# FNet and GEGLU layers on one core: when the last pair's wide tiles of x are loaded, and when the late norms run

## The chip, the core and the metric

The kernel runs on one core of a Trainium2 chip. Its time is the device time of one launch in microseconds; the median of three runs of the kernel before is 1612.08 us (1611.62 to 1616.12). TensorE (PE) multiplies, VectorE (DVE) and ScalarE (ACT) do the elementwise work, GpSimd (POOL) issues stores and some loads, and SyncE (SP) issues most loads. Each of these engines takes its instructions in the order in which they stand in its own program.

## What is computed

```python
x = A_x                                     # [1, 2048, 512], float32
for layer in range(2):
    z = layernorm(x)                        # over the 512 columns
    a = z @ dft_hid_re.T
    b = z @ dft_hid_im.T
    x = x + (dft_seq_re @ a - dft_seq_im @ b)       # FNet mixing, 2048 x 2048 matrices
    z = layernorm(x)
    x = x + (gelu(z @ w_gate) * (z @ w_up)) @ w_down  # GEGLU, 512 -> 1792 -> 512
```

The kernel counts these as four layers: 0 and 2 mix, 1 and 3 are GEGLU. The change lies at the end of layer 2 and the beginning of layer 3.

## The kernel before

Every matmul is of float32 data cut into a high and a low half, so each product of 128 x 128 by 128 x 512 is three matmuls (L227 high by high, L228 high by low, L229 low by high). ACT makes the high half of an operand (L170, or L196 on another form), DVE the low half (L172, L198). A product can start when ACT's half is there, and its second matmul when DVE's is. Both matrix stages are done by seven-product schemes, so sums of blocks (L203, L207, L210 on DVE) stand ahead of many splits. PSUM has eight banks, which ACT copies out (L214) or copies to another bank as a seed (L221).

The 2048 rows of x are four blocks of 512. Data sits in 98 slots of 128 x 512 in SBUF, and in two wide tiles of 1 MB, `wide` and `xwide`, each of which holds one block. In layer 2 the blocks are worked in pairs, (0, 1) and (2, 3). A block's stages are S2 and S4, sequences of matmul steps over the sequence dimension; its matrices stream through the slots as loads `s<-ws` on SP, and the hidden matrices as `s<-wq`. After S4 of the second block of a pair the products of the pair with the hidden matrices follow; `PAIR_REST`, twelve of them, makes the last ones. For the last pair these twelve are put aside in `spare`, and layer 3 runs them one by one beside its own first passes. Their results are turned by L865 and added into the wide tiles (L210), which must hold the old x by then, and `pair_out` (L980) stores the tiles as the next layer's x. `pair_wide_load` (L977) loads a wide tile from x in four pieces, on SP. For the last pair, `xwide` is loaded in S2 of block 3 at step 14 and `wide` in S4 at step 5 (`WIDE_AT`). For the first pair both are loaded before its products.

Layer 3 starts with half of x (blocks 0 and 1) normed in turn: `z^T` of these rows must be there. That is done inside layer 2, since x of blocks 0 and 1 is known. A row tile is loaded ("L" in `NORM_STEPS`, L255 or L264), its mean and variance are taken on DVE (L645, L647, "A"), POOL makes the reciprocal root (L652), DVE the shift (L656), ACT norms (L689), and DVE turns it into `wide` (L782, "B"). After four tiles POOL stores `wide` to a scratch tensor t (L785), and the same queue fetches z^T back in pieces of 64 KB (L796, `s<-t`). Tiles 4 to 7 come first; tiles 0 to 3 are the four late ones. `NORM_STEPS` says which of these parts run at which step, `NORM_LATE` the parts that go to the head of the queue of S2 of block 3, and the fetches follow after `FETCH_AT` queue steps:

```python
queue.extend(late + [None] * (FETCH_AT - len(late) if paired else 14)
             + [run for fetch in later.pop("fetches") for run in (None, fetch)])
```

The code's order sets what is issued first on each engine only in part: a scheduler orders the instructions within their dependences. SP takes loads one after the other; a load goes out when its slot is free, and with eight loads under way it waits for the oldest. Layer 3's first weights are the loads `s<-wb` (L1345), in high and low halves.

## Time and profile before

| | |
|---|---|
| median of the runs | 1612.08 us (1611.62 to 1616.12, 3 runs) |
| profiled execution | 1612.12 us; its span is 1610.3 us, mean clock of TensorE 0.994 |
| busy | PE 1592.9 us, DVE 1189.7, ACT 880.8, POOL 315.6 |
| DMA | 432.80 MB, 269 GB/s over the span |

A busy PE isn't PE at its peak: a matmul counts as busy also when the clock is halved. So PE's time is read by stretches, from the granted clock, the number of matmuls and the waits. A wait is named by what came last: `PE p L227 <- ACT s L170` means that the matmul of line 227 waited for a split of line 170. DMA share is the busy share of the 16 DMA engines, and can pass 1.00 a little.

### The profile page before, as it was taken

What the parts mean: (1) busy time and instruction counts of PE and PEld (TensorE: products, weight loads), DVE (VectorE), ACT (ScalarE), POOL (GpSimd) and SP (SyncE); (2) the same over time, 40 slices, a digit from 0 to 9 for tenths busy, and PEclk for the clock granted to TensorE, in tenths of its full rate; (3) what the DMA queues carried; (4) which work ended last, traced back from release to release, by engine and by line L of the source; (5) the groups of instructions that cost most, each with busy time, mean ns of one, the idle gap of its engine ahead of it and who ended that gap; (6) DMA issues with size and microseconds to landing.
All of it is one profiled execution on the core that took longest, in us unless ns stands there. A gap on an engine that the chain in (4) does not pass through costs nothing. (4 is left out here: it accounts for less than half of the span.)

```text
span 1610.3 us, 22765 instructions
## 1 busy us (share of the span) xinstructions
PE 1592.9 (99%) x6960; PEld 1311.8 (81%) x6960; DVE 1189.7 (74%) x2082; ACT 880.8 (55%) x1687; POOL 315.6 (20%) x533
## 2 busy tenths in 40 slices
PE   9999999999999999999999999999989999999999
PEld 7888888888888888888888888887768888888887
DVE  7997888878699784675878875998875556843574
ACT  8955565654767644656567543534542565433460
POOL 4122332341456102330040000022301000000000
PEclk9999999999999999999999999999889999999999
DMA  9888999976998899997786758789868958895445
GB/s 358 293 329 314 332 318 345 334 260 199 343 322 318 267 333 314 326 353 225 273 303 199 262 166 206 240 279 271 236 231 285 280 171 252 302 293 188 131 144 157
DMA packets 245019, 432.80 MB, mean 269 GB/s; under 512 B 29024, under 2 KB 72288, under 8 KB 243872
## 3 DMA queue, kind: packets, MB, share of 16 engines
q1 hardware_dynamic: 212208, 328.82, 63.6%
q0 software_dynamic: 30000, 100.43, 17.4%
q10 hardware_dynamic: 2688, 2.10, 0.5%
q8 instruction: 55, 0.90, 0.2%
q14 instruction: 68, 0.56, 0.1%
HBM read 333.97 MB, written 97.26 MB: 268 GB/s over the span
## 5 line engine op out<-in xcount | busy, mean ns | idle before, releaser
L228 PE MATMUL p<-s,s 128*128 128x512 f32 x2304 | 897.2, 390 | 0.6 <-DVE s L172 0.5
L229 PE MATMUL p<-s,s 128*128 128x512 f32 x2304 | 891.5, 390 | 3.5 <-DMA s<-wb 3.5
L227 PE MATMUL p<-s,s 128*128 128x512 f32 x2304 | 852.5, 391 | 8.3 <-ACT s L170 3.7
L170 ACT ACTIVATE s<-s 128x512 fp32r<-128x512 f32 (+1 forms) x852 | 480.4, 608 | 305.7 <-DVE s L203 69.7
L172 DVE TENSOR_TENSOR s<-s,s 128x512 fp32r<-128x512 f32 (+1 forms) x852 | 537.6, 663 | 119.5 <-ACT s L170 101.5
L227 PEld LDWEIGHTS p<-s,s 128*128 128x128 f32 x2304 | 434.2, 189 | 100.7 <-ACT s L170 4.7
L229 PEld LDWEIGHTS p<-s,s 128*128 128x128 f32 x2304 | 434.4, 189 | 94.1 <-DMA s<-wb 3.9
L228 PEld LDWEIGHTS p<-s,s 128*128 128x128 f32 x2304 | 434.1, 188 | 92.8 <-DVE s L172 2.2
L207 DVE TENSOR_TENSOR s<-s,p 128x512 f32<-128x512 f32 x211 | 142.3, 682 | 163.7 <-PE p L229 133.5
L203 DVE TENSOR_TENSOR s<-s,s 128x512 f32<-128x512 f32 (+1 forms) x399 | 234.6, 609 | 5.8 <-DMA s<-ws 3.2
L214 ACT ACTIVATE s<-p 128x512 f32<-128x512 f32 x234 | 135.6, 592 | 112.9 <-PE p L229 110.8
L1355 ACT ACTIVATE s<-s 128x512 f32<-128x512 f32 x84 | 52.8, 628 | 46.3 <-DVE s L207 45.9
L336 POOL DMA_DIRECT2D wb<-s x84 | 46.1, 550 | 86.2 <-ACT s L170 68.4
L1355 ACT ACTIVATE s<-p 128x512 f32<-128x512 f32 x28 | 16.7, 596 | 83.1 <-PE p L229 81.5
L689 ACT ACTIVATE s<-s,shift,rstd 128x512 f32<-128x512 f32 x61 | 48.8, 810 | 18.3 <-DVE shift L656 10.4
L1371 DVE TENSOR_TENSOR s<-s,p 128x512 f32<-128x512 f32 x56 | 38.3, 683 | 24.8 <-PE p L229 24.8
L980 POOL DMA_DIRECT2D x<-wide x8 | 5.2, 658 | 231.1 <-DVE wide L210 231.1
L221 ACT ACTIVATE p<-p 128x512 f32<-128x512 f32 x56 | 32.6, 584 | 31.6 <-PE p L229 31.4
L170 ACT ACTIVATE s<-xwide 128x512 fp32r<-128x512 f32 (+1 forms) x56 | 34.3, 618 | 27.9 <-DVE xwide L207 10.4
L210 DVE TENSOR_TENSOR s<-s,s 128x512 f32<-128x512 f32 (+1 forms) x61 | 36.4, 603 | 17.1 <-DMA s<-ws 12.4
L172 DVE TENSOR_TENSOR s<-xwide,s 128x512 fp32r<-128x512 f32 (+1 forms) x56 | 37.4, 676 | 15.3 <-ACT s L170 15.1
L666 POOL TENSOR_SCALAR rstd<-rstd 128x1 f32<-128x1 f32 x32 | 19.8, 619 | 108.1 <-ACT s L665 98.8
(96 smaller groups left out, 675.1 us busy)
## 6 DMA issues: line engine op xcount, KB each, us to landing
s<-ws SPq DMA_DIRECT2D x368, 256.0 KB, 5.0
s<-wb SPq DMA_DIRECT2D x294, 256.0 KB, 5.0
s<-wc SPq DMA_DIRECT2D x182, 256.0 KB, 4.4
wb<-s POOLq DMA_DIRECT2D x98, 256.0 KB, 4.6
s<-wq SPq DMA_DIRECT2D x56, 256.0 KB, 4.5
s<-x SPq DMA_DIRECT2D x52, 256.0 KB, 5.4
s<-wh SPq DMA_DIRECT2D x52, 256.0 KB, 5.6
wc<-s POOLq DMA_DIRECT2D x49, 256.0 KB, 5.4
```

What stands on the lines that cost most here:

```text
L170: newest["ACT"] = nc.scalar.activation(hi, src, AF.Copy)
L172: newest["DVE"] = nc.vector.tensor_tensor(lo, src, f32(hi), op=ALU.subtract)
L203: nc.vector.tensor_tensor(out, a, b, op=ALU.subtract)
L207: bank_read["DVE"] = nc.vector.tensor_tensor(out, a, b, op=ALU.add)
L214: bank_read["ACT"] = nc.scalar.activation(v, src, AF.Copy)
L227: nc.tensor.matmul(ps, ah, bh, start=start, stop=False, skip_group_check=True)
L228: nc.tensor.matmul(ps, ah, bl, start=False, stop=False, skip_group_check=True)
L229: newest["PE"] = nc.tensor.matmul(ps, al, bh, start=False, stop=stop, skip_group_check=True)
L336: nc.gpsimd.dma_start(a, f32(t))
L689: nc.scalar.activation(z, x, AF.Identity, bias=shift, scale=rstd)
L1355: nc.scalar.activation(t, g, AF.Gelu_apprx_tanh)
L1371: nc.vector.tensor_tensor(t, t, v, op=ALU.mult)
```

## The change

```diff
@@ -27,7 +27,7 @@
 MORE = 8
 RAW = 4
 FETCHING = 2
-WIDE_AT = 14, 5
+WIDE_AT = 0, 2
 IN_ORDER = (3, 0),
 HELD = {0: (1, 2, 3), 2: ()}
 WARM = 12
@@ -50,11 +50,11 @@
 BESIDE = 2
 FURTHER = 4
 NORM_STEPS = (
-    (("A", 4),), (("A", 5),), (("B", 4), ("A", 6)), (("B", 5), ("A", 7)), (("B", 6),), (("B", 7),), (), (),
-    (("L", 0),), (("L", 1),), (("L", 2),), (("L", 3),),
+    (("A", 4),), (("A", 5),), (("B", 4), ("A", 6)), (("B", 5), ("A", 7)), (("B", 6),), (("B", 7),),
+    (("L", 0),), (("L", 1),), (("L", 2),), (("L", 3),), (), (("A", 0),), (("A", 1),), (("A", 2),),
 )
-NORM_LATE = ("A", 0), ("A", 1), ("A", 2), ("A", 3), ("B", 0), ("B", 1), ("B", 2), ("B", 3)
-FETCH_AT = 12
+NORM_LATE = ("A", 3), ("B", 0), ("B", 1), ("B", 2), ("B", 3)
+FETCH_AT = 10
 FIRST_SUMS = 9, 10
 LATER = 3
 LET = 5
@@ -1027,6 +1027,9 @@
         def pair_rest(i):
             if sums_due:
                 pair_sums()
+            if pair_now[0][1] == NB - 1 and i in WIDE_AT:
+                which = 1 - WIDE_AT.index(i)
+                pair_wide_load(pair_now[0][which], which)
             if i in FIRST_SUMS:
                 first_sum(FIRST_SUMS.index(i))
             pair_product(*PAIR_REST[i])
@@ -1160,8 +1163,6 @@
                     pair_rest(j // BESIDE)
                     if j == len(skewed(3)) // 2:
                         stream["more"] = FURTHER
-                if last and paired and j == WIDE_AT[0]:
-                    pair_wide_load(NB - 2, 0)
                 if i == 0:
                     six(chain, "T2", k, False, k == NK - 1)
                 elif i == 1:
@@ -1198,8 +1199,6 @@
             one, three = sides.pop(b)
             u = us.pop(b)
             for j, (i, k) in enumerate(skewed(2)):
-                if last and paired and j == WIDE_AT[1]:
-                    pair_wide_load(NB - 1, 1)
                 if i == 0:
                     six(one, "B22", k, False, k == NK - 1, "22" if last else None)
                 else:

```

The two loads of wide tiles leave S2 and S4 of block 3 and go to the twelve products that were put aside, `wide` to the first of them and `xwide` to the third. The loads of the four late row tiles come two steps sooner, the first three statistics move from the late list into the steps, the late list is three entries shorter and the fetches stand two steps sooner.

**SP, the loads ahead of layer 3.** Names are tile<-tensor with their numbers; `wb` are layer 3's weights, `wq` the hidden matrices, `ws` those of the sequence. Before, `wide` stands among the loads of S4:

```order
L350 DMA s_12951<-wq_183 128x512
L350 DMA s_12907<-ws 128x512
L350 DMA s_12894<-ws 128x512
L977 DMA wide<-x_3_95 32x16x128
L350 DMA s_12919<-ws 128x512
L977 DMA wide<-x_3_95 32x16x128 x3
L350 DMA s_12966<-wq_184 128x512
L350 DMA s_12978<-wq_183 128x512
```

and `xwide` among those of S2:

```order
L350 DMA s_12578<-ws 128x512
L350 DMA s_12650<-wq_181 128x512
L977 DMA xwide<-x_2_94 32x16x128 x4
L350 DMA s_12677<-wq_182 128x512
L350 DMA s_12576<-ws 128x512
```

Now both stand behind layer 3's first weights:

```order
L1344 DMA s_13101<-wb_185 128x512
L350 DMA s_13172<-wq_184 128x512
L1344 DMA s_13122<-wb_186 128x512
L350 DMA s_13154<-wq_183 128x512
L977 DMA wide<-x_3_95 32x16x128 x4
L350 DMA s_13291<-wc_122 128x512
L350 DMA s_13303<-wq_183 128x512
L1344 DMA s_13247<-wb_187 128x512
L1344 DMA s_13248<-wb_187 128x512
L350 DMA s_13309<-wq_184 128x512
L350 DMA s_13317<-wq_182 128x512
L350 DMA s_13315<-wq_181 128x512
```

The late low half that PE's second matmul of layer 3 takes is `s_13101<-wb_185` here. Between it and the first wq_184 load of S4 stand 21 loads; before, 18 stood between the like loads. A few rows earlier on SP the first two `L255 s<-x_0` of the late norms now come directly behind `s_12412<-ws`, with five `ws` loads behind them; before, `s_12348<-ws` and `s_12318<-ws` and others stood ahead.

**DVE, the late norms.** Around the first late transpose (L782), in S2 of block 3; L172 is the low half of a split, L203 and L210 are sums of blocks. Before:

```order
L651 TENSOR_SCALAR rstd<-mv 128x1
L210 TENSOR_TENSOR s_12576<-s_12574,s_12576 128x512
L203 TENSOR_TENSOR s_12529<-s_12527,s_12529 128x512
L651 TENSOR_SCALAR rstd<-mv 128x1 x2
L203 TENSOR_TENSOR s_12574<-s_12578,s_12574 128x512
L172 TENSOR_TENSOR s_12680<-s_12576,s_12679 128x512
L172 TENSOR_TENSOR s_12598<-s_12529,s_12597 128x512
L203 TENSOR_TENSOR s_12578<-s_12576,s_12578 128x512
L172 TENSOR_TENSOR s_12714<-s_12574,s_12713 128x512
L656 SCALAR_TENSOR_TENSOR shift<-mv,rstd 128x1
L782 STREAM_TRANSPOSE wide<-s_12541 128x16x32
```

Now, with the next norm's statistics ahead of it and the second transpose a dozen rows on:

```order
L656 SCALAR_TENSOR_TENSOR shift<-mv,rstd 128x1
L172 TENSOR_TENSOR s_12437<-s_12352,s_12436 128x512
L645 BN_STATS st<-s_12346 128x6
L645 BN_STATS st<-s_12364 128x6
L782 STREAM_TRANSPOSE wide<-s_12502 128x16x32
L172 TENSOR_TENSOR s_12542<-s_12318,s_12541 128x512
L210 TENSOR_TENSOR s_12537<-s_12535,s_12537 128x512
L203 TENSOR_TENSOR s_12490<-s_12488,s_12490 128x512
L172 TENSOR_TENSOR s_12510<-s_12412,s_12509 128x512
L172 TENSOR_TENSOR s_12685<-s_12580,s_12684 128x512
L203 TENSOR_TENSOR s_12728<-s_12728,s_12322 128x512
```

The transpose that stood behind all sums of this step now stands ahead of several (`s_12537`, `s_12490`), and the other three follow sooner as well.

**PE, the first products of layer 3.** `p_13285` before and `p_13280` now is the bank that ACT copies (L214) in the middle of its chain, `p_13334` and `p_13329` the one whose copy (L221) seeds the next. Before, the end of the first part and what follows:

```order
L229 MATMUL p_13285<-s_13194,s_13119 128x512
L227 MATMUL p_13285<-s_13208,s_13118 128x512
L228 MATMUL p_13285<-s_13209,s_13118 128x512
L229 MATMUL p_13285<-s_13208,s_13119 128x512
L227 MATMUL p_13285<-s_12994,s_13122 128x512
L228 MATMUL p_13285<-s_12995,s_13122 128x512
L229 MATMUL p_13285<-s_12994,s_13122 128x512
L227 MATMUL p_13285<-s_13026,s_13122 128x512
```

The matmul on `s_12994` waits for the copy. Now:

```order
L228 MATMUL p_13280<-s_13199,s_13108 128x512
L229 MATMUL p_13280<-s_13198,s_13109 128x512
L227 MATMUL p_13336<-s_12869,s_13114 128x512
L228 MATMUL p_13336<-s_12870,s_13114 128x512
L229 MATMUL p_13336<-s_12869,s_13115 128x512
L227 MATMUL p_13336<-s_12873,s_13114 128x512
L228 MATMUL p_13336<-s_12874,s_13114 128x512
L229 MATMUL p_13336<-s_12873,s_13115 128x512
L227 MATMUL p_13329<-s_13082,s_13118 128x512
L228 MATMUL p_13329<-s_13083,s_13118 128x512
L229 MATMUL p_13329<-s_13082,s_13119 128x512
L227 MATMUL p_13329<-s_13092,s_13118 128x512
```

The matmul that waits for the copy comes behind two more on `p_13329`, so twelve stand between where none did. And between the start of this chain and the end of its first part stand fourteen matmuls on `p_13226` and `p_13227`, where two on `p_13236` and `p_13237` stood. On ACT the copy has seven splits ahead of it now, and had eight.

## The prediction

> **What bounds the kernel now.** I read the page first: how full TensorE is, and where its clock falls.

> ```profile
> span 1610.3 us, 22765 instructions
> PE 1592.9 (99%) x6960; PEld 1311.8 (81%) x6960; DVE 1189.7 (74%) x2082; ACT 880.8 (55%) x1687; POOL 315.6 (20%) x533
> PEclk9999999999999999999999999999889999999999
> ```

> PE is busy 99% of the span, so only its idle time and its slow clock can be won. Each of the 40 slices is 40.3 us long; the two 8s in the clock row stand at 1127 to 1208 us, the only dip. Next, the waits of PE over the whole program (us in total, times, longest):

> ```profile
> PE p L227 <- ACT s L170: 3.7, 2, 3.3
> PE p L229 <- DMA s<-wb: 3.5, 1, 3.5
> PE p L227 <- ACT s L214: 3.0, 2, 2.3
> ...
> PE p L227 <- DMA s<-wb: 1.6, 1, 1.6
> ...
> PE p L228 <- DVE s L172: 0.5, 1, 0.5
> ```

> 12.3 us in all, nearly all in that dip. To price a stall with the slow clock behind it, I take windows: from the moment at which the next matmul was due to the first one at full clock again. The columns are length, then busy time with count for PE, PEld, DVE, ACT and POOL, then clock, DMA share, GB/s. The last row is an undisturbed stretch.

> ```profile
> 1124.47:1137.54 13.07, 9.26 (x21) 6.28 (x21) 9.49 (x21) 6.30 (x10) 7.13 (x12) 0.61 0.65 192
> 1170.67:1181.77 11.10, 5.97 (x16) 4.33 (x16) 9.58 (x17) 3.06 (x6) 0.00 (x0) 0.69 0.87 322
> 1192.01:1198.64 6.63, 4.37 (x12) 3.30 (x12) 5.67 (x10) 4.11 (x8) 0.00 (x0) 0.74 0.22 59
> 600.00:700.00 100.00, 100.00 (x442) 82.79 (x442) 57.18 (x99) 51.06 (x110) 29.57 (x47) 1.00 0.98 321
> ```

> In each row one matmul had begun before the window. So full pitch is 100/441 = 0.2268 us, and the losses are 13.07 − 20 × 0.2268 = **8.53**, 11.10 − 15 × 0.2268 = **7.70** and 6.63 − 11 × 0.2268 = **4.14 us**. Together 20.4 us, 1.3% of the time: the most that this change can win, since it touches nothing else.

> **Stall 1 (1124 to 1137 us).** The split that PE waits for stands on ACT behind a split of a sum that DVE had not made, because DVE waited for a load:

> ```profile
> 1125.86 0.69 DVE L210 TENSOR_TENSOR s<-s,s 128x512 f32<-128x512 f32 x1 [5.13 <-DMA s<-ws]
> ...
> 1112.79 2.02 SPq L977 DMA_DIRECT2D xwide<-x  x4
> ...
> s<-ws SPq DMA_DIRECT2D x3, 256.0 KB, 10.2
> DMA packets 1852, 0.98 MB, mean 195 GB/s; under 512 B 60, under 2 KB 1824, under 8 KB 1851
> ...
> s<-ws SPq DMA_DIRECT2D x6, 256.0 KB, 5.9
> DMA packets 1443, 3.41 MB, mean 379 GB/s; under 512 B 164, under 2 KB 164, under 8 KB 1314
> ```

> The first pair of DMA rows is of 1115 to 1120 us, right behind the four xwide loads; the second of 1096 to 1105 us. With nearly all packets under 2 KB the engines move 195 GB/s instead of 379, and a ws load takes 10.2 us to land instead of 5.9. The change takes the xwide loads out of this queue. The load then lands 4 us or more sooner, and DVE no longer stops. What is late next is DVE itself, and the norms that now come sooner:

> ```profile
> 1096.00:1138.63 42.63, 38.42 (x149) 29.90 (x148) 35.31 (x70) 19.91 (x35) 12.31 (x21) 0.88 0.79 231
> L782 DVE STREAM_TRANSPOSE wide<-s 128x512 f32<-128x512 f32 x8 | 5.7, 710 | 1.9 <-ACT s L689 1.7
> L656 DVE SCALAR_TENSOR_TENSOR shift<-mv,rstd 128x1 f32<-128x1 f32 x8 | 1.1, 150 | 0.0
> L689 ACT ACTIVATE s<-s,shift,rstd 128x512 f32<-128x512 f32 x8 | 6.3, 808 | 1.8 <-DVE shift L656 1.8
> ```

> From 1096 us to the end of the last late transpose DVE is idle for 42.63 − 35.31 = 7.3 us, and all its work there stays. So the stretch can shrink by 7.3 us at most. By the order, the first two norms now stand among the splits that PE takes before the stall. They put 2 × 0.71 (L782) + 2 × 0.15 (L656) = 1.7 us on DVE and 2 × 0.81 = 1.6 us on ACT (L689) ahead of those splits, in an in-order chain where each can hold the other. 7.3 − 1.7 − 1.6 = **4.0 us won**, bounds 0 (a new wait of the same size) and 7.3. I take 4.0, since both delays come from measured durations. The BN_STATS stood ahead of the stall already and cost nothing new.

> **Stall 2 (1171 to 1182 us).** PE waits 1.6 and then 3.5 us for the first pieces of layer 3's weights, a high half and the low half that belongs to it.

> ```profile
> wide<-x SPq DMA_DIRECT2D x4, 256.0 KB, 7.2
> 1140.00:1178.00 38.00, 32.87 (x142) 26.64 (x142) 36.26 (x60) 17.29 (x32) 9.30 (x17) 0.96 1.05 307
> 1128.00:1140.00 12.00, 11.44 (x31) 8.19 (x32) 9.70 (x20) 7.49 (x12) 3.61 (x7) 0.62 0.47 139
> 1140.13 0.61 POOL L785 DMA_DIRECT2D t<-wide  x1 [8.52 <-DVE wide L782]
> 1147.61 4.34 POOL L796 DMA_DIRECT2D s<-t  x8 [6.87 <-issue]
> DMA packets 1911, 3.48 MB, mean 387 GB/s; under 512 B 211, under 2 KB 211, under 8 KB 1911
> 1177.12 0.79 PE L229 MATMUL p<-s,s 128*128 128x512 f32 x1 [3.48 <-DMA s<-wb]
> ```

> The DMA engines are full from 1140 to 1178 us (share 1.05): the four wide loads and the second fetch of z^T share the start of it, and the weights land in single file behind them, at 387 GB/s (row of 1168 to 1177 us), 0.26 MB/387 = 0.68 us each. Before, from 1128 to 1140 us, the share is 0.47. Two things relieve this. The wide loads leave: 1.05 MB at the 195 GB/s of small packets is 5.4 us (2.7 at 387). And the last transpose frees the store of z^T, the store frees the fetch, so both come sooner by the 4.0 us of stall 1 and by two to three queue steps, into engines that had been half idle; relative to PE I count 3 us. Against that, the late weight piece now stands behind three loads more in SP's row: 3 × 0.68 = 2.0. Relief 5.4 + 3 − 2.0 = 6.4 us, against 1.6 + 3.5 = 5.1 of waits: the DMA wait goes. What is late next is DVE again, busy 36.26 of 38.00 us there; I leave two instructions at L782's 0.71 us for it. 7.70 − 1.4 = **6.3 us won**, bounds 0 and 7.7.

> **Stall 3 (1192 to 1199 us).**

> ```profile
> 1194.42 0.50 PE L227 MATMUL p<-s,s 128*128 128x512 f32 x1 [2.26 <-ACT s L214]
> 1189.61 4.27 ACT L170 ACTIVATE s<-s 128x512 fp32r<-128x512 f32 x8
> 1193.78 0.59 ACT L214 ACTIVATE s<-p 128x512 f32<-128x512 f32 x1
> ```

> The copy that PE needs stands on ACT behind eight splits, 0.53 us each. In the new order seven splits stand ahead of it still, but PE has 12 matmuls more ahead of the end of the part that is copied, and 12 more between that end and the matmul that needs the copy: 24 × 0.2268 = 5.4 us of other work against a wait of 2.26. What is late next is L221's copy into the next bank, behind the same splits, with about nothing to spare; I leave one ACT instruction, 0.6 us. 4.14 − 0.6 = **3.5 us won**, bounds 0 and 4.1.

> **Costed at nothing.** The eight x loads in their new place:

> ```profile
> 1180.00:1210.00 30.00, 27.74 (x112) 22.30 (x111) 21.66 (x36) 16.53 (x32) 0.00 (x0) 0.92 0.56 169
> 1209.16 1.25 DVE L210 TENSOR_TENSOR wide<-wide,s 128x512 f32<-128x512 f32 x2
> 1211.55 1.25 DVE L210 TENSOR_TENSOR xwide<-xwide,s 128x512 f32<-128x512 f32 x2
> ```

> DMA has 0.44 × 30 = 13 us free from 1180 us on, against 2 × 5.4 that the loads need, and the tiles are first read at 1209 and 1211 us. Were that cover gone, DVE would stop in order at L210.

> **Sum.** 4.0 + 6.3 + 3.5 = 13.8 us off the profiled run's 1612.1 (its median of the runs is the same to 0.1): **1598.3 us**. With every bound at its best 7.3 + 7.7 + 4.1 = 19.1 are won, 1593.0.

> [...]

> **Rivals.** (1) *The weights stay DMA-bound.* If the packets' size is not what slows the wide loads, their leaving saves 2.7 us, and the three loads ahead take 2.0 back. Then the late piece lands only 0.7 us sooner by the clock, and what stall 1 gave is waited for again: 1612.1 − 0.7 − 3.5 = 1607.9. For it: share 1.05. Against: the 195 GB/s. (2) *A new short wait drops the clock.* The norms that come sooner leave several waits of about a microsecond. Behind stall 1's two waits (3.3 and 0.5) the clock cost another 8.53 − 3.8 = 4.8 us: 1598.3 + 4.8 = 1603.1. (3) *The stalls only move*, DVE being the bound of the whole stretch: 1612. Against: its 7.3 us of idle. (4) *Slower: the early row loads stop SP's queue.*

> ```profile
> 1082.37 2.61 POOL L980 DMA_DIRECT2D x<-xwide  x4
> x<-xwide POOLq DMA_DIRECT2D x4, 256.0 KB, 8.0
> 1092.96 0.33 SPq L255 DMA_DIRECT2D s<-x  x1
> ```

> The rows of x that the late norms read are written by stores issued from 1082.37 to 1084.98, which take 8.0 us. Today SP comes to the first such load at 1092.96, when they have landed. Two steps sooner SP comes there with the stores still under way, and five ws loads stand behind it. If these land as late as the worst of this trace, 10.2 − 5.9 = 4.3 us late, DVE, which has no idle time there, stops PE, with the clock's 4.8 behind it: 9.1 lost. It turns the sign once stall 2 also stays as in rival 1: 1612.1 + 9.1 − 0.7 − 3.5 = 1617.0. Against: three of the ws loads were moved ahead of the row loads.

> **Numbers.** Forecast 0.55, rival 1 0.15, rival 2 0.17, rival 3 0.06, rival 4 0.07. Rival 1 lies at the edge of what this kernel's runs can tell from no change, 0.3% or 4.8 us, so half of it counts to each side: faster 0.79, within 0.14, slower 0.07. The range runs from 1592 (all bounds at their best) to 1611, which leaves out rivals 3 and 4.

> **What would show it.** Right: no clock dip at 1124 to 1137, no wait of PE on wb, the copy of L214 no longer waited for, ws loads landing in 3 to 6 us, the second store of z^T near 1132 us, the wide loads landing long before L210. Wrong: a PE wait between 1095 and 1110 us on ws sums (rival 4), the wait on wb still there (rival 1), or small waits of ACT and DVE followed by half clock (rival 2).

## The result, and the profile after

| | before | changed |
|---|---|---|
| median | 1612.73 us (1611.62 to 1616.12, 4 runs) | 1601.99 us (1600.46 to 1602.35, 4 runs) |
| profiled execution, span | 1610.3 us | 1600.2 us |

The ratio is 0.9928 (95% interval 0.9911 to 0.9945): the change makes the kernel 10.7 us faster by the medians, 10.1 by the profiled spans. Forecast were 1598.3 us and 13.8 us won.

The page of the changed kernel, the lines that were shown of before:

```profile
span 1600.2 us, 22754 instructions
PE 1588.2 (99%) x6960; PEld 1306.1 (82%) x6960; DVE 1188.5 (74%) x2082; ACT 880.3 (55%) x1687; POOL 317.0 (20%) x533
PEclk9999999999999999999999999999999999999999
```

The two 8s in the clock row are gone. The waits of PE from 1095 to 1260 us (us in total, times, longest):

```profile
PE p L228 <- DVE s L172: 2.2, 2, 1.6
PE p L227 <- DVE s L207: 1.2, 2, 0.9
PE p L229 <- DMA s<-wb: 1.0, 1, 1.0
PE p L227 <- ACT s L170: 0.6, 2, 0.3
```

5.0 us where there were 11.6. ACT's copy (L214) is no longer waited for, the weights for 1.0 us instead of 5.1, and DVE has become the engine that is waited for most. The windows of what is left, cut as in the prediction, with one matmul in each count begun before:

```profile
1109.65:1117.75 8.10, 5.87 (x16) 3.91 (x16) 7.09 (x16) 5.09 (x10) 1.73 (x2) 0.79 0.66 229
1126.61:1130.40 3.79, 3.06 (x12) 2.09 (x12) 3.79 (x9) 1.71 (x3) 3.58 (x6) 1.00 0.82 244
1169.20:1174.05 4.85, 2.86 (x10) 1.64 (x10) 4.85 (x10) 2.00 (x5) 0.00 (x0) 1.00 1.08 350
1180.00:1200.00 20.00, 20.00 (x90) 16.57 (x89) 20.00 (x35) 12.68 (x24) 0.00 (x0) 1.00 1.08 287
```

Losses are 8.10 − 15 × 0.2268 = 4.70 us, 3.79 − 11 × 0.2268 = 1.30 and 4.85 − 9 × 0.2268 = 2.81; in the last row, where stall 3 would be, PE is busy all of 20 us. The first one is new: before, this place lost 0.7. What makes it is read backwards. PE waits for splits, DVE for a ws load, and SP had stood still (timeline rows of PE, DVE and SP, and the waits of SP's queue from 1080 to 1110 us):

```profile
1110.13 1.25 PE L227 MATMUL p<-s,s 128*128 128x512 f32 x4 [0.33 <-ACT s L170]
1111.69 0.73 PE L227 MATMUL p<-s,s 128*128 128x512 f32 x2 [0.30 <-ACT s L170]
1114.01 0.79 PE L228 MATMUL p<-s,s 128*128 128x512 f32 x1 [1.59 <-DVE s L172]
...
1110.66 0.69 DVE L210 TENSOR_TENSOR s<-s,s 128x512 f32<-128x512 f32 x1 [1.27 <-DMA s<-ws]
...
1084.21 1.92 SPq L350 DMA_DIRECT2D s<-ws  x2
1094.18 0.80 SPq L255 DMA_DIRECT2D s<-x  x2
1095.08 2.95 SPq L350 DMA_DIRECT2D s<-ws  x5
...
SPq L255 <- DMA x<-xwide: 7.8, 1, 7.8
```

The row loads (L255) that the change puts two steps sooner came to SP at about 1086 us and waited 7.8 us for the stores of the rows they read. The ws loads behind them went out from 1095 us on, next to the 1 MB store of z^T (issued at 1099.44, 9.0 us to landing). DVE, which works without a pause there (busy 4.39 of 4.39 us from 1105.00 on), met one that had not landed at 1109.39: it had gone out at 1101.43 and took 9.1 us. Three short waits of PE follow, and then half clock (the mean of the window is 0.79). This is rival 4 of the prediction, at about half of its price, and beside rival 2.

### The profile page after: what moved, and what is told of

Its sections match the earlier page's. It is cut to its first block, busy times and chain, and to the rows that moved or that the text cites. A ratio compares the mean times of both kernels' runs of the same rounds, so it can differ in the third digit from the quotient of the medians.

```text
span 1600.2 us, 22754 instructions
## 1 busy us (share of the span) xinstructions
PE 1588.2 (99%) x6960; PEld 1306.1 (82%) x6960; DVE 1188.5 (74%) x2082; ACT 880.3 (55%) x1687; POOL 317.0 (20%) x533
## 4 chain that ended last, share of the span: by engine, by line
PE 92%; DVE 3%; DMA 2%; POOL 1%; issue 1%; ACT 0%; SPq 0%; DVEq 0%; POOLq 0%; ACTq 0%
PE p L228 31%; PE p L229 31%; PE p L227 31%; DVE s L172 2%; PE p L1094 1%; DVE s L203 1%; DMA s<-ws 1%; POOL s L796 0%; DMA t<-wide 0%; DMA xwide<-ws 0%; DMA s<-wb 0%; DMA s<-x 0%; DMA s<-t 0%; POOL rstd L666 0%; POOL rstd L652 0%
## 5 line engine op out<-in xcount | busy, mean ns | idle before, releaser
L228 PE MATMUL p<-s,s 128*128 128x512 f32 x2304 | 895.6, 390 | 3.2 <-DVE s L172 3.0
L229 PE MATMUL p<-s,s 128*128 128x512 f32 x2304 | 889.4, 389 | 1.0 <-DMA s<-wb 1.0
L227 PE MATMUL p<-s,s 128*128 128x512 f32 x2304 | 849.4, 390 | 2.6 <-DVE s L207 1.2
L170 ACT ACTIVATE s<-s 128x512 fp32r<-128x512 f32 (+1 forms) x852 | 480.1, 608 | 295.2 <-DVE s L203 70.1
L172 DVE TENSOR_TENSOR s<-s,s 128x512 fp32r<-128x512 f32 (+1 forms) x852 | 536.8, 661 | 119.6 <-ACT s L170 101.8
L228 PEld LDWEIGHTS p<-s,s 128*128 128x128 f32 x2304 | 433.0, 188 | 96.0 <-DVE s L172 5.9
L227 PEld LDWEIGHTS p<-s,s 128*128 128x128 f32 x2304 | 432.4, 188 | 95.5 <-ACT s L170 2.8
L229 PEld LDWEIGHTS p<-s,s 128*128 128x128 f32 x2304 | 433.0, 188 | 91.1 <-DMA s<-wb 1.4
L207 DVE TENSOR_TENSOR s<-s,p 128x512 f32<-128x512 f32 x211 | 142.0, 682 | 159.6 <-PE p L229 130.8
L203 DVE TENSOR_TENSOR s<-s,s 128x512 f32<-128x512 f32 (+1 forms) x399 | 234.4, 607 | 4.8 <-DMA s<-ws 2.3
L214 ACT ACTIVATE s<-p 128x512 f32<-128x512 f32 x234 | 135.3, 592 | 113.8 <-PE p L229 112.0
L689 ACT ACTIVATE s<-s,shift,rstd 128x512 f32<-128x512 f32 x61 | 48.7, 809 | 19.8 <-DVE shift L656 12.4
L210 DVE TENSOR_TENSOR s<-s,s 128x512 f32<-128x512 f32 (+1 forms) x61 | 36.5, 602 | 20.5 <-DMA s<-ws 16.7
L980 POOL DMA_DIRECT2D x<-wide x8 | 5.2, 659 | 226.6 <-DVE wide L210 226.6
L170 ACT ACTIVATE s<-xwide 128x512 fp32r<-128x512 f32 (+1 forms) x56 | 34.2, 617 | 28.0 <-DVE xwide L207 8.2
L172 DVE TENSOR_TENSOR s<-xwide,s 128x512 fp32r<-128x512 f32 (+1 forms) x56 | 37.4, 675 | 16.3 <-ACT s L170 16.1
L221 ACT ACTIVATE p<-p 128x512 f32<-128x512 f32 x56 | 32.6, 584 | 27.7 <-PE p L229 27.6
L666 POOL TENSOR_SCALAR rstd<-rstd 128x1 f32<-128x1 f32 x32 | 19.1, 598 | 111.3 <-ACT s L665 104.3
## 6 DMA issues: line engine op xcount, KB each, us to landing
s<-ws SPq DMA_DIRECT2D x368, 256.0 KB, 5.2
s<-wb SPq DMA_DIRECT2D x294, 256.0 KB, 5.4
s<-wc SPq DMA_DIRECT2D x182, 256.0 KB, 4.6
wb<-s POOLq DMA_DIRECT2D x98, 256.0 KB, 4.8
s<-wq SPq DMA_DIRECT2D x56, 256.0 KB, 5.3
s<-x SPq DMA_DIRECT2D x52, 256.0 KB, 5.4
s<-wh SPq DMA_DIRECT2D x52, 256.0 KB, 5.6
wc<-s POOLq DMA_DIRECT2D x49, 256.0 KB, 5.4
```

What stands on the lines that cost most here:

```text
L170: newest["ACT"] = nc.scalar.activation(hi, src, AF.Copy)
L172: newest["DVE"] = nc.vector.tensor_tensor(lo, src, f32(hi), op=ALU.subtract)
L203: nc.vector.tensor_tensor(out, a, b, op=ALU.subtract)
L207: bank_read["DVE"] = nc.vector.tensor_tensor(out, a, b, op=ALU.add)
L214: bank_read["ACT"] = nc.scalar.activation(v, src, AF.Copy)
L227: nc.tensor.matmul(ps, ah, bh, start=start, stop=False, skip_group_check=True)
```

## The experiments

The losses of PE, in us, are added up from the gaps between the starts of its matmuls beyond the pitch. Stall 1 counts from 1105 to 1148 us, the new one included, stall 2 up to the first products of layer 3, stall 3 behind it; the last column is the stretch from 1095 to 1260 us.

| kernel | median us | ratio to before | stall 1 | stall 2 | stall 3 | stretch |
|---|---|---|---|---|---|---|
| before | 1612.3 to 1612.7 | | 9.2 | 7.7 | 4.2 | 21.1 |
| changed | 1601.99 | 0.9928 (0.9911 to 0.9945) | 6.5 | 2.9 | 0 | 9.3 |
| the same again | 1603.09 | 0.9939 (0.9926 to 0.9952) | 7.0 | 6.6 | 0 | 13.6 |
| wide loads only | 1601.73 | 0.9936 (0.9921 to 0.9951) | 2.5 | 2.9 | 4.1 | 10.1 |
| norms only | 1609.93 | 0.9986 (0.9973 to 0.9999) | 5.6 | 10.7 | 1.6 | 17.9 |
| xwide only | 1607.49 | 0.9968 (0.9957 to 0.9979) | 1.9 | 9.8 | 4.2 | 15.9 |
| wide only | 1604.94 | 0.9955 (0.9939 to 0.9972) | 6.5 | 2.1 | 2.5 | 11.0 |
| rows later | 1604.22 | 0.9944 (0.9923 to 0.9965) | 8.9 | 3.3 | 1.0 | 13.1 |
| rows on POOL | 1599.35 | 0.9914 (0.9894 to 0.9935) | 4.9 | 2.1 | 0 | 7.0 |
| the same again | 1601.42 | 0.9934 (0.9921 to 0.9946) | 6.1 | 2.9 | 0 | 9.0 |
| fetches 4 sooner | 1601.36 | 0.9921 (0.9899 to 0.9944) | 4.3 | 4.2 | 0 | 8.5 |
| 32 rows, 8 KB | 1610.12 | 0.9982 (0.9971 to 0.9993) | 5.8 | 10.1 | 4.2 | 20.1 |
| 128 rows, 512 B | 1609.42 | 0.9982 (0.9973 to 0.9991) | 6.6 | 5.2 | 4.2 | 15.9 |
| 128 rows, 2 KB | 1606.75 | 0.9970 (0.9957 to 0.9983) | 3.7 | 7.1 | 4.2 | 14.9 |

The two lines of the changed kernel show how little one profile says: the same program lost 2.9 or 6.6 us in stall 2, while its medians agree. The losses are of one profile each, so differences of a few us between two lines are hints unless several kernels agree.

### Which part of the change does it

First the change is taken apart. Wide loads only: the norms as before.

```diff
-    (("L", 0),), (("L", 1),), (("L", 2),), (("L", 3),), (), (("A", 0),), (("A", 1),), (("A", 2),),
+    (), (), (("L", 0),), (("L", 1),), (("L", 2),), (("L", 3),),
-NORM_LATE = ("A", 3), ("B", 0), ("B", 1), ("B", 2), ("B", 3)
-FETCH_AT = 10
+NORM_LATE = ("A", 0), ("A", 1), ("A", 2), ("A", 3), ("B", 0), ("B", 1), ("B", 2), ("B", 3)
+FETCH_AT = 12
```

> Only the two wide loads are moved to the put-aside products; the norms and fetches stand as before. Theory A (the small-packet loads of the wide tiles cause stalls 1 and 2, and the sooner row loads cost the 4.9 us that the changed kernel newly loses at 1110 us): stall 1 vanishes with no new stall in its place, no clock dip before 1140 us, the wait on wb is shorter than 3.5 us; about 1597 us, faster than the changed kernel by some 4 us. Theory B (the gain needs the norms, since DVE and the fetch of z^T set the pace): the wait on wb stays at 3 us or more with half clock behind it, and the time is 1604 to 1608 us, slower than the changed kernel.

Measured 1601.73 us, the time of the whole change. PE's waits from 1080 us on:

```profile
PE p L227 <- ACT s L214: 2.2, 1, 2.2
PE p L229 <- DMA s<-wb: 1.8, 1, 1.8
PE p L228 <- DVE s L172: 1.5, 1, 1.5
PE p L227 <- ACT s L170: 0.4, 1, 0.4
```

No stall at 1110 us, stall 1 down to 2.5 us, the wait on wb at 1.8: theory A's picture, theory B is out. But the time isn't 1597, since stall 3 is still there (2.2 us of wait and half clock behind it): what the norms cost in stall 1, they win in stall 3.

Norms only: the other half, the wide loads in their old places.

```diff
-NORM_LATE = ("A", 0), ("A", 1), ("A", 2), ("A", 3), ("B", 0), ("B", 1), ("B", 2), ("B", 3)
-FETCH_AT = 12
+NORM_LATE = ("A", 3), ("B", 0), ("B", 1), ("B", 2), ("B", 3)
+FETCH_AT = 10
```

(and `NORM_STEPS` as in the change)

> Only the norms and the fetches come sooner; the wide loads stand as before. Theory A: a new stall of about 5 us near 1110 us, and stalls 1 and 2 stay (their loads are still behind the wide tiles), so 1612 to 1618 us. Theory B: the fetch that comes sooner relieves stall 2, 1604 to 1608 us.

Measured 1609.93 us, 2.5 us faster by the medians: between the two expectations. Stalls 1 and 2 stay in another form, and stall 3 shrinks to 1.6 us. The place at 1110 us lost only 2.2 us, not the 5 that theory A expected, although SP stood still here too:

```profile
SPq L255 <- DMA x<-xwide: 7.2, 1, 7.2
```

One tile at a time, with the norms as before (the edit for xwide against the changed kernel, shortened; the one for wide mirrors it):

```diff
-            if pair_now[0][1] == NB - 1 and i in WIDE_AT:
-                which = 1 - WIDE_AT.index(i)
-                pair_wide_load(pair_now[0][which], which)
+            if pair_now[0][1] == NB - 1 and i == WIDE_AT[1]:   # xwide only
+                pair_wide_load(pair_now[0][0], 0)
...
+                if last and paired and j == 5:                 # wide in S4, as before
+                    pair_wide_load(NB - 1, 1)
```

> Only xwide is moved, wide is loaded in S4 as before, the norms as before. Theory A: stall 1 vanishes and stall 2 stays at 6 to 10 us: 1602 to 1606 us. Theory B (DVE is the bound of the stretch, the loads only shift where PE waits): under 4 us won, 1609 us or more.

> Only wide is moved, xwide is loaded in S2 as before, the norms as before. Theory A: stall 1 stays at 8 to 9 us, the wait on wb shrinks to under 1.5 us without half clock: 1603 to 1607 us. Theory B: the wait on wb stays above 3 us: 1609 us or more.

Measured 1607.49 us with xwide moved (5.0 us won) and 1604.94 with wide moved (7.5 won). Each removes its own stall: xwide stall 1 (1.9 us left), wide stall 2 (2.1 left). With xwide alone, stall 2 grew from 7.7 to 9.8 us, since PE came to it sooner and the DMA did not: part of what stall 1 gave was waited for again, as rival 1 of the prediction has it. So 1607.49 is above the range expected. With wide alone stall 1 was 5.8 us, where 8 to 9 were expected, behind a wait of 2.6 us and with the clock at full speed all through (mean 1.000); the last section comes back to it.

### The stall that the sooner row loads make

Rows later: the changed kernel with the row loads at their old steps.

```diff
-    (("A", 4),), (("A", 5),), (("B", 4), ("A", 6)), (("B", 5), ("A", 7)), (("B", 6),), (("B", 7),),
-    (("L", 0),), (("L", 1),), (("L", 2),), (("L", 3),), (), (("A", 0),), (("A", 1),), (("A", 2),),
+    (("A", 4),), (("A", 5),), (("B", 4), ("A", 6)), (("B", 5), ("A", 7)), (("B", 6),), (("B", 7),), (), (),
+    (("L", 0),), (("L", 1),), (("L", 2),), (("L", 3),), (("A", 0),), (("A", 1),),
-NORM_LATE = ("A", 3), ("B", 0), ("B", 1), ("B", 2), ("B", 3)
+NORM_LATE = ("A", 2), ("A", 3), ("B", 0), ("B", 1), ("B", 2), ("B", 3)
```

> The changed kernel with the four row loads back at their old steps (on SP behind the ws loads, as before the change), the first two statistics behind them and the fetches two steps sooner as in the change. Theory A (the row loads that come sooner stop SP's queue and so make the new stall at 1110 us): no wait on ws sums near 1110 us, under 1 us lost there instead of 4.7. The copy that makes stall 3 stands one matmul ahead of its reader in this order, so stall 3 (4 us) is back if theory A is right that it goes by the order alone: about 1601 us. Theory B (the norms themselves on DVE and ACT make the new stall): 4 us or more are still lost between 1107 and 1120 us, and the time is 1604 us or more.

Measured 1604.22 us. The place at 1110 us lost 1.1 instead of 4.7, near what theory A says; but 7.8 us were lost at 1131 to 1144, in waits of PE on splits (4.0 us there) and the half clock behind them, so that the time is where theory B put it, though not the place. DVE had waited 2.7 us for a ws load there (until 1131.55); why that load was late is open. And the copy was waited for only 0.7 us: with PE so late, ACT had caught up. So theory A's first number was missed narrowly, the other two clearly.

Rows on POOL: the changed kernel, and POOL issues the row loads. The order is the same on PE and ACT but for a swap or two; on DVE about a dozen instructions around the late norms change places.

```diff
-                    both.update({("L", i): lambda i=i: ahead(i, 1, nc.sync) for i in range(NT)})
+                    both.update({("L", i): lambda i=i: ahead(i, 1, nc.gpsimd) for i in range(NT)})
```

> The changed kernel with the four row loads issued by POOL instead of SP; the order on PE, ACT and DVE is that of the changed kernel nearly everywhere. Theory A (SP's stopped queue makes the new stall): the ws loads no longer stand behind the stores, the stall at 1110 us shrinks from 4.7 to under 2 us, and the time is 1597 to 1599 us, faster than the changed kernel. Theory B (norms on DVE and ACT make it): 1602 us, the stall stays.

> The changed kernel with the row loads on POOL, again. Theory A (the stopped SP queue makes the stall at 1110 us): 2 to 4 us faster than the changed kernel of the same call. Theory B (chance between runs): within 1 us of it.

> The changed kernel again, beside the one with the row loads on POOL: 1601 to 1602 us.

SP's queue ran on in both kernels with the row loads on POOL. What is left of the stall in the first (timeline rows of SP, DVE and PE):

```profile
1084.08 17.59 SPq L350 DMA_DIRECT2D s<-ws  x14
...
1107.37 0.69 DVE L210 TENSOR_TENSOR s<-s,s 128x512 f32<-128x512 f32 x1 [0.49 <-DMA s<-ws]
...
1108.40 1.26 PE L227 MATMUL p<-s,s 128*128 128x512 f32 x4 [0.33 <-ACT s L170]
1109.96 0.73 PE L227 MATMUL p<-s,s 128*128 128x512 f32 x2 [0.30 <-ACT s L170]
1123.55 0.50 PE L228 MATMUL p<-s,s 128*128 128x512 f32 x1 [1.59 <-DVE s L172]
```

The wait on DVE at 1114 us is gone, and with it the half clock: 1.6 us are lost near 1110 us, and 1.4 in the second run, against 4.7 and 5.2 of the changed kernel. That SP's stopped queue makes that stall is shown twice. The three profiles in which it stopped agree: 7.2 us (norms only), 7.8 and 8.5 us (the changed kernel, twice) cost 2.2, 4.7 and 5.2 us, the first without half clock. But a wait of the same size on DVE stands some 14 us later, where DVE is behind all the same, with a loss of 2.8 and 4.3 us where the changed kernel lost 1.3 twice. Whether the whole is faster is not settled: 1599.35 and 1601.42 us against 1601.99 and 1603.09, with intervals that overlap. Of the times expected, that of the first run with rows on POOL was missed by 0.4 us. In the second comparison the difference is 1.7 us, between the two theories, and the changed kernel came 1.1 us above its range.

### Stall 3

Fetches 4 sooner: wide loads moved, norms and rows as before, `FETCH_AT` 8.

```diff
-FETCH_AT = 12
+FETCH_AT = 8
```

> The wide loads moved as in the change, the norms and row loads as before, and the fetches four queue steps sooner. In its order the copy that made stall 3 has 20 matmuls between it and its reader, where the wide loads moved alone have 2. Theory A (stall 3 hangs on that distance alone): stall 3 vanishes, stall 1 stays under 2 us as with the loads alone, 1596 to 1598 us. Theory B (stall 3 is ACT's load of splits, whatever the distance): a wait on the copy or its neighbours of 2 us or more remains, 1601 us.

Measured 1601.36 us; stall 3 is gone, as theory A says, but stall 1 is 4.3 us instead of 2.5, and stall 2 is 4.2. The time is the one of the wide loads alone: the order moved the loss. By the orders, no matmul stands between the end of the part that is copied and the reader of the copy in six kernels that keep stall 3 at 4.1 or 4.2 us (and in a seventh, wide only, with 2.5). Twelve stand there in the changed kernel and the two with rows on POOL, and eighteen in this one (the text above counts two more), and none of these has it. Two kernels show that the distance isn't all. Norms only has the twelve too and lost 1.6 us, in a wait of 1.3 us for the copy into the next bank (L221). Rows later has none and lost 1.0 us, since PE came late. In the changed kernel ACT's rows stand as before, with PE elsewhere meanwhile:

```profile
1183.36 3.76 ACT L170 ACTIVATE s<-s 128x512 fp32r<-128x512 f32 x7
1187.01 0.59 ACT L221 ACTIVATE p<-p 128x512 f32<-128x512 f32 x1
1189.00 0.60 ACT L214 ACTIVATE s<-p 128x512 f32<-128x512 f32 x1 [1.40 <-PE p L229]
```

Seven splits and then the copies; now ACT waits for PE at L214, not PE for ACT.

### What makes the wide loads dear

Three kernels leave everything as before and change only the shape of the last pair's wide loads, at the same place and with the same bytes. The edits are shortened here, one comment for each kernel. They leave the rows of x in other places of the tiles, so only their times are of use.

```diff
-                moved(pair_wide[n], xs[layer, b], lambda v, rows: nc.sync.dma_start(v, rows))
+    # 32 rows, 8 KB:   pair_wide[n][p * 32:(p + 1) * 32]   <- xs[layer, b][p * P:(p + 1) * P].rearrange("(t j) e -> t (j e)", j=NT)
+    # 128 rows, 512 B: pair_wide[n][:, q * TB:(q + 1) * TB].rearrange("t (j e) -> t j e", e=P)
+    #                     <- xs[layer, b].rearrange("(j t) (q e) -> q t j e", t=P, e=P)[q]
+    # 128 rows, 2 KB:  pair_wide[n][:, q * TB:(q + 1) * TB] <- xs[layer, b][q * P:(q + 1) * P]
```

> The kernel before, its two wide loads where they were, with the same bytes in rows of 8 KB per partition instead of 512 B (the rows of x land in other places of the tile, so the last two blocks of layer 2 are added to the wrong rows). Theory A (small packets are what makes these loads dear): the DMA engines move over 350 GB/s behind xwide instead of 195, the ws load behind it lands in under 7 us instead of 10.2, stall 1 shrinks below 3 us and the wait on wb below 2 us: 1598 to 1604 us. Theory C (their bytes and their place in SP's queue do it): stalls 1 and 2 stay within 2 us of what they were, 1609 us or more.

> The kernel before, its two wide loads in place, each piece of 256 KB spread over all 128 partitions instead of 32, still in runs of 512 B (the rows of x land in other places of the tile, so the last two blocks of layer 2 are added to the wrong rows). With rows of 8 KB over 32 partitions the engines moved no more than 221 to 256 GB/s behind xwide, so the size of packets is not what makes these loads dear. [...] Theory A (packets of 512 B): stall 1 stays at 8 us and the rate at 195 GB/s.

> As the run with all 128 partitions, but in runs of 2 KB, the shape of every other load of this kernel (again the last two blocks of layer 2 get the wrong rows of x). [...] Theory A: only this one is faster than the kernel before, by 4 us or more.

Four windows of 4 us, each from 2.2 us behind the first xwide issue (the last number is GB/s). Before:

```profile
1115.00:1119.00 4.00, 4.00 (x19) 3.33 (x18) 4.00 (x9) 0.63 (x1) 3.80 (x7) 1.00 1.08 194
```

32 partitions in runs of 8 KB:

```profile
1116.20:1120.20 4.00, 4.00 (x19) 3.34 (x18) 4.00 (x9) 0.63 (x1) 3.80 (x7) 1.00 0.99 211
```

128 partitions in runs of 512 B, and in runs of 2 KB:

```profile
1115.40:1119.40 4.00, 4.00 (x19) 3.31 (x18) 4.00 (x9) 0.63 (x1) 3.80 (x7) 1.00 1.06 302
```

```profile
1115.00:1119.00 4.00, 4.00 (x19) 3.34 (x18) 4.00 (x11) 0.64 (x1) 3.77 (x7) 1.00 0.98 329
```

The engines are full in all four (share 0.98 to 1.08). Runs sixteen times as long bring 211 GB/s instead of 194; all 128 partitions bring 302, still with 512 B, and 329 with 2 KB. The ws load behind xwide took 10.2, 9.3, 7.5 and 6.5 us to land in these four. So it is the 32 partitions of a load that cost, and the size of the packets only a little; the number of packets under 2 KB on which the prediction leaned only came with it. Why 32 partitions cost so much, no run shows. The times fit less well: 2.5, 2.9 and 5.5 us are won. The 2 KB runs are ahead of those of 512 B by 2.7 us by the medians, and that only they win 4 us or more is what theory A said. The intervals of the two overlap, so the rates and the landings decide here, not the times.

## Why the prediction was right, step by step

**What bounds the kernel.** Right: all that was won came out of the three stalls. In the profiled runs the stretch lost 21.1 us before and 9.3 after, so 11.8 were won, and some 1.5 us went to short waits between 900 and 1080 us, where the order of work hadn't changed (the same program lost 0.1 there the second time): 10.1 to 10.3 in the span.

**Stall 1: 4.0 us forecast, 2.7 measured** (9.2 to 6.5). The mechanism was right for the loads: xwide taken away alone leaves 1.9 us, so 7.3 were to be had, as much as DVE's idle time allowed. What was subtracted for the norms was of the right order, 3.3 against 4.0 us (6.5 less the 2.5 of the wide loads alone), but its make-up was not, so that the two lie close is luck. I counted their work on DVE and ACT and left out SP's queue, stopped for 7.8 us. The prediction had this as rival 4, with 9.1 us and a chance of 0.07; it came in with 1.27 us of DVE's time and the clock behind it, 4.7 us in all. Its price for the clock, 4.8 us, was that of stall 1, where the clock was halved for 10.24 us; here it was halved for 3.41. How the 4.0 us divide is not settled: where SP's queue ran on, stall 1 still lost 4.9 and 6.1.

**Stall 2: 6.3 forecast, 4.9 and 1.1 us measured in the two profiles.** The wait on the weights shrank from 5.1 us to 1.0 in one and 2.0 in the other, but did not go, as this step said it would: the DMA engines are still full there (share 1.08 at 1169 to 1174 us). DVE's L207 came in as forecast, 1.2 us both times. Most of the 3.7 us between the two profiles is half clock, 6.83 us of it behind the wait of 2.0. Mis-sized is the relief from the fetches: I counted 3 us, and norms and fetches alone left stall 2 at 10.7 us (with stall 1 3.6 us shorter). The second store of z^T came at 1138.24 us and not near 1132; with the wide loads alone, and the norms as before, it came at 1136.03. So the norms that start sooner did not end sooner. Rows of POOL and DVE in the changed kernel show why:

```profile
1124.57 3.83 POOL L796 DMA_DIRECT2D s<-t  x7 [10.21 <-DVE mv L647]
1128.59 0.55 POOL L796 DMA_DIRECT2D s<-t  x1 [0.19 <-issue]
1129.15 4.76 POOL L652 TENSOR_TENSOR rstd<-rstd,power 128x1 f32<-128x1 f32 x2
1133.88 4.37 POOL L796 DMA_DIRECT2D s<-t  x8
1138.24 0.57 POOL L785 DMA_DIRECT2D t<-wide  x1
...
1133.43 0.16 DVE L656 SCALAR_TENSOR_TENSOR shift<-mv,rstd 128x1 f32<-128x1 f32 x1 [0.46 <-POOL rstd L652]
1134.48 1.42 DVE L782 STREAM_TRANSPOSE wide<-s 128x512 f32<-128x512 f32 x2 [0.21 <-ACT s L689]
```

The last transpose that is stored ends at 1135.90. It had waited for POOL's two roots, which stand between sixteen issues of fetches and took 4.8 us; why so long, where two of them took 1.07 and 1.06 us in the kernel before (at 1085.00 and 1089.73), no run shows. The store then stands behind the last eight issues for 2.3 us more. The step named the queue of SP and left out POOL's. And the wide loads' dearness was put down to small packets, where it is the 32 partitions (302 GB/s with the same 512 B over 128); the number, 195 GB/s, held.

**Stall 3: 3.5 forecast, 4.2 measured.** Right, and mainly for the reason given: the distance between the copy and its reader. The 0.6 us left for L221's copy were not needed here; norms only shows that wait (1.3 us). With the wide loads moved, stall 3 is the only thing for which the norms and fetches were good, and the fetches alone, put sooner, do it too.

**Costed at nothing.** Right: in the changed kernel DVE waits nowhere for the wide tiles.

**Rivals.** Rival 1 came true in part where xwide alone was moved: of 7.3 us won in stall 1, 2.1 were lost again at the weights. Its condition, that the packets' size is not what slows the wide loads, holds (211 against 194 GB/s), but they were slow all the same. Rival 2's half clock came at 1114 us, behind rival 4's wait. Rival 3 came in part: with rows on POOL, or with the fetches sooner, what one place won was partly lost at the next, because DVE has little to spare there (in the changed kernel it was busy 3.79 of 3.79 us at 1126.61 and 4.85 of 4.85 at 1169.20).

**The sum** was 13.8 us, 11.8 in the stretch of the first profile and 7.5 in the second: the error is stall 1's clock and queue, and stall 2's fetches. All three signs of being wrong that the prediction named were there, each smaller than priced: a wait for a ws load near 1110 us, a wait on wb, and half clock behind short waits.

## What to carry to other kernels

When a load comes sooner, look at what it waits for itself: here it stopped all that stood behind it on SP's queue for 7.8 us (1086 to 1094), and the price was paid some twenty microseconds later on another engine (PE's waits from 1110 to 1114). Take an edit apart before praising it: here two moved loads made the whole gain, and the four edits beside them traded one stall for another. And spread a load over all partitions where the layout allows it (the DMA engines moved 302 GB/s here where they moved 194 with 32), or keep it out of the stretches where the DMA engines are full.

## What the runs showed of the hardware

While the DMA engines were full of wide loads and what stood behind them, they moved 194 and 211 GB/s with each load on 32 partitions, and 302 and 329 with each on 128. The longer runs brought 9% in both cases.

```profile
1123.51:1126.92 3.41, 1.11 (x5) 0.57 (x4) 1.06 (x2) 0.34 (x1) 2.65 (x5) 1.00 1.02 265
1126.92:1137.16 10.24, 8.72 (x19) 5.97 (x20) 8.05 (x18) 5.87 (x9) 4.69 (x8) 0.50 0.59 179
1171.29:1174.70 3.41, 1.17 (x4) 0.67 (x4) 3.41 (x7) 0.70 (x2) 0.00 (x0) 1.00 1.05 387
1174.70:1181.53 6.83, 4.41 (x10) 3.46 (x11) 5.38 (x9) 1.71 (x3) 0.00 (x0) 0.50 0.80 295
1191.77:1195.18 3.41, 1.15 (x5) 0.66 (x4) 3.41 (x6) 3.09 (x7) 0.00 (x0) 1.00 0.27 94
1195.18:1198.60 3.42, 3.42 (x9) 2.65 (x9) 2.50 (x5) 1.26 (x2) 0.00 (x0) 0.50 0.23 41
...
1110.64:1114.05 3.41, 1.51 (x6) 0.64 (x5) 3.39 (x10) 2.11 (x4) 1.42 (x2) 1.00 0.86 316
1114.05:1117.46 3.41, 3.41 (x8) 2.76 (x9) 3.41 (x6) 1.73 (x3) 0.31 (x1) 0.50 0.35 96
```

And two steps around each of the two waits. Both loads moved:

```profile
1180.10:1183.51 3.41, 1.21 (x5) 0.68 (x5) 3.41 (x7) 3.29 (x7) 0.00 (x0) 1.00 1.14 240
1183.51:1186.92 3.41, 3.41 (x9) 2.64 (x8) 3.41 (x6) 0.00 (x0) 0.00 (x0) 0.50 1.19 188
```

Wide only:

```profile
1181.64:1185.05 3.41, 2.86 (x13) 2.05 (x11) 3.41 (x6) 3.41 (x8) 0.00 (x0) 1.00 1.03 378
1185.05:1188.46 3.41, 1.76 (x8) 1.46 (x9) 3.41 (x7) 2.08 (x5) 0.00 (x0) 1.00 0.54 169
```

The wait with both loads moved falls into one step, in which PE idles 3.41 − 1.21 = 2.20 us, and the next step is at half clock. The one of wide only is cut by the end of a step into 0.55 and 1.65 us, and nothing follows. The wait of 2.6 us in stall 1 of the same kernel is cut too (1.73 and 1.93 us busy). In the profiles of before and of the changed kernel, four steps at full clock had more than 1.3 us without a busy PE (2.30, 2.24, 2.26 and 1.90 us, in the rows above), and half clock followed each; the others had up to 1.27, and it followed none. In the changed kernel it was two waits, of 0.30 and 1.59 us, that left 1.51 us of busy time in the step from 1110.64 us; the first of the three at 1110 us had ended before. With rows on POOL, waits of 1.59 and 0.61 us left the clock alone in the first run (mean clock of the profiled run 1.000), and 1.62 and 0.62 halved it in the second (0.998). Each step at half clock costs up to half of 3.41 us, 1.7 us, by an estimate from these records. So in these profiles a step with 1.68 us without a busy PE (wide only, 3.41 − 1.73) kept the clock, and one with 1.90 (changed) lost it; the ends of matmuls are modelled in them.
